# Scores of the last 64 keys as float32 products of two pairs at once

## The chip, the core and the metric

The kernel runs on one core of one Trainium2 chip. The metric is the device time of one execution in microseconds (us), lower is better. The engines are TensorE (PE for its products, PEld for its loads of weights into the array), ScalarE (ACT), VectorE (DVE), GpSimd (POOL, hardly used here) and SyncE (SP), which issues nearly all DMA transfers.

## The reference

Attention with a sigmoid in place of the softmax, then two matrix products with a leaky ReLU between them. There are 8 batches of 12 heads, 448 tokens and 64 values per head; d_model is 768 and d_ff is 2048.

```python
scores = scale * np.matmul(q, k.transpose(0, 1, 3, 2)) - np.log(S)
attn = 1.0 / (1.0 + np.exp(-scores))
attn_out = np.matmul(attn, v)
x = attn_out.transpose(0, 2, 1, 3).reshape(B * S, H * D)
h = x @ w_in
out = np.maximum(0.01 * h, h) @ w_out
```

## The kernel before

**Two kinds of product.** Most operands are float32 values that are split in two: a high part of type float32r, made by a cast on ACT (sometimes DVE), and a low part, the value minus its high part, made by a subtraction on DVE. A product of two split operands is three float32r products: high by high, high by low and low by high. The products of the sigmoids with v are not split: both operands are plain float32, and each such product shows as two instructions in the profile.

**The attention stage** works on 48 pairs of heads (`Pair`, line 343). The 128 partitions of a pair's tile hold the 64 head values of its two heads, so a score product needs only half of the array's rows, and the two heads of a pair run in the two halves side by side. The 448 keys of a head are four chunks: three of 128 and one of 64. For each chunk six score products (three for each of two heads) fill a tile of PSUM, `sc`, of two banks, one for each head. ACT takes the sigmoid of it into a tile `s`. There are three such PSUM tiles (tag `s` of `ps_a`), and five tiles for sigmoids (pool `at`).

The last chunk has only 64 keys. An even pair (`part` 1) writes its scores to partitions 0 to 63 of its tile, an odd pair (`part` 2) to partitions 64 to 127 of another tile, for which it multiplies 128 keys and uses 64. Both sigmoids go to one tile `s`, so that the last keys of two pairs can be multiplied with v together: four float32 products, each in its own quarter of the array (64 rows by 64 columns), in `attn_v` of the odd pair.

**Order of the work.** The order of instructions on every engine is the order in which the program issues them. The program runs in slots: `slot` (line 108) first issues the chores that are due (`later`), then the slot's own products. Step j of the attention stage has four slots: the last two chunks of pair j's scores (`scores(1)`), the first two chunks of pair j+1 (`scores(0)`), then the products with v for chunks 0 and 1 (`attn_v(0)`) and for the rest (`attn_v(1)`). Chores of step j: the split of pair j+2 (`high` on ACT, or on DVE where ACT has another cast in that slot, and `low` on DVE), the load of v for pair j+2, and the load of q and k for pair j+4. These loads go to the pool `raws`, which has two tiles; the parts go to the pool `spl`, two tiles as well. The results of two pairs are copied from PSUM by ACT (`keep`) in the first slot behind the odd pair. Beside all this DVE prepares the weights (`prep`), a given number of operations in each slot, and at given slots (`PLAN_ATTN`) parts of the attention output are split for the stage that follows (`h` high, `l` low, `s` sum; "h602" is the high part of operand 6, all three blocks).

**The product stages** multiply the four quarters of the tokens with `w_in` and later with `w_out`, by a scheme of seven products for a two by two block product (`ORDER`, `Quad`). A quarter of the first one is 56 steps of nine products, eight groups of seven operands in the order 0, 1, 4, 5, 3, 6, 2. The operands of quarter p+1 are split while quarter p is multiplied, in steps named by `PLANS` ("p50" is step 50 of the quarter before, "np0" step 0 of the quarter itself).

**Places.** Operands and parts lie in tiles of one size, handed out by `take` from two lists, `left` and `right`, oldest first. The attention stage has LEFT = 10 left and RIGHT = 14 right tiles. When its own pools are closed, MORE = 4 left tiles are made in their place and join the end of the left list.

Of the kernel before, what the change touches and what calls it, by code (L numbers as in the profile page):

```python
# [9 lines left out]
F32 = mybir.dt.float32  # L10
F32R = mybir.dt.float32r
I32 = mybir.dt.int32
AF = mybir.ActivationFunctionType
# [3 lines left out]
P = 128  # L17
# [3 lines left out]
NOP = len(ORDER)  # L21
# [9 lines left out]
IDLE = 7  # L31


LEFT, MORE, RIGHT = 10, 4, 14


def part(i):
# [14 lines left out]
def attn_ffn_kernel(ctx: ExitStack, tc: tile.TileContext, qk, v, w_in, w_out, out):  # L52
# [13 lines left out]
    S = qk.shape[3]  # L66
    NP = qk.shape[0] // B
    D = P // 2
    NK = 4
# [4 lines left out]
    NQ = B // 2  # L74
    scale = 1.0 / math.sqrt(D)
    bias = -math.log(S)
    heads = [slice(j * D, j * D + D) for j in range(2)]
# [9 lines left out]
    mm, dma = pinned(nc.tensor.matmul), pinned(nc.sync.dma_start)  # L87
    copy, act, dma_act = (pinned(x) for x in (nc.scalar.copy, nc.scalar.activation, nc.scalar.dma_start))
# [3 lines left out]
    def sub(to, x, y):  # L92
        vec(out=to, in0=x, in1=y, op=ALU.subtract)
# [64 lines left out]
    class Quad:  # L158
# [14 lines left out]
        def take(self, what, acc, how=copy):  # L173
            t = self.pool.tile([P, S], F32, tag=self.tag, name=f"{what}_{self.name}", bufs=self.bufs)
            how(out=t, in_=acc[:, :S])
            return t
# [30 lines left out]
    ps = ExitStack()  # L207
# [22 lines left out]

    def tiles(stack, name, side, n):
        pool = stack.enter_context(tc.tile_pool(name=name, bufs=1, side=side, reuse_waits="tile"))
        free[side].extend((pool, f"{name}{i}", side) for i in range(n))

    taken = {}

# [10 lines left out]
    def give(name):  # L247
# [5 lines left out]
    tiles(left, "l", "left", LEFT)  # L253
    attn = ExitStack()
    raws, spl, at = (attn.enter_context(tc.tile_pool(name=name, bufs=bufs, reuse_waits="tile")) for name, bufs in (
        ("raws", 2), ("spl", 2), ("at", 5)))
    warm = shift(ctx, "warm", 32, "right")
    tiles(right, "r", "right", RIGHT)
    pp = right.enter_context(tc.tile_pool(name="pp", bufs=2, side="right"))
# [80 lines left out]
    HALVES = slice(0, S // 2), slice(S // 2, S)  # L340
    KEYS = slice(0, 2 * P), slice(2 * P, S)

    class Pair:


# [22 lines left out]

        def high(self, how=None):
            self.parts = spl.tile([P, 2, 2, S], F32R, tag="qks", name=f"qks_{self.i}")  # L370
            (how or copy)(out=self.parts[:, 0], in_=self.raw)

        def low(self):
            sub(self.parts[:, 1], self.raw, self.parts[:, 0])

        def split(self):

            self.parts = spl.tile([P, 2, 2, S], F32R, tag="qks", name=f"qks_{self.i}")
            high, low = self.parts[:, 0], self.parts[:, 1]
            for cols in HALVES:  # L380
                copy(out=high[:, 0, cols], in_=self.raw[:, 0, cols])
            for n, cols in enumerate(KEYS):
                vcopy(out=high[:, 1, cols], in_=self.raw[:, 1, cols])
                sub(low[:, 1, cols], self.raw[:, 1, cols], high[:, 1, cols])
                if n == 0:
                    for x in HALVES:
                        sub(low[:, 0, x], self.raw[:, 0, x], high[:, 0, x])

        def scores(self, h):
            todo, acts = [], []  # L390
            for c in range(2 * h, 2 * h + 2):
                ps = psum("s", f"sc_{self.i}_{c}")

                if c < NK - 1:
                    k0, n, rows = c * P, P, slice(0, P)
                elif self.part == 1:
                    k0, n, rows = S - D, D, slice(0, D)
                else:
                    k0, n, rows = S - P, P, slice(D, P)

                for cols in HALVES if self.i == h == 0 else (slice(0, S),):
                    for m, (kp, qp) in enumerate(((0, 0), (0, 1), (1, 0))):
                        for j, me in enumerate(heads):
                            todo.append((c, (m > 0 and c + 1, m, cols.start), dict(
                                out=ps[:n, j, cols], lhsT=self.parts[me, kp, 1, k0:k0 + n],
                                rhs=self.parts[me, qp, 0, cols], start=m == 0 and cols.start == 0,
                                stop=m == 2 and cols.stop == S, skip_group_check=True)))
                acts.append((c, rows, ps))
            if self.i == h == 0:
                todo.sort(key=lambda x: x[1])  # L410
            for n, (c, rows, ps) in enumerate(acts):
                for x in todo if self.i == h == 0 and n == 0 else [x for x in todo if x[0] == c and (self.i or h)]:
                    mm(**x[2])
                if self.part == 2 and c == NK - 1:
                    s = pairs[self.i - 1].a[c]
                else:
                    s = at.tile([P, 2, S], F32, tag="s", name=f"s_{self.i}_{c}")
                act(out=s[rows], in_=ps[rows, :, :S], func=AF.Sigmoid, bias=bias, scale=scale)
                self.a.append(s)

        def attn_v(self, h):
            if h == 0:
                self.pv = psum("pv", f"pv_{self.i}")
            for c in range(2 * h, min(2 * h + 2, NK - 1)):
                for j, me in enumerate(heads):
                    mm(self.pv[me, :S], lhsT=self.v[:, (NK - 1) * j + c, :], rhs=self.a[c][:, j], start=c == 0, stop=False,
                       skip_group_check=True)
            if h == 1 and self.part == 2:
                x = pairs[self.i - 1]
                for j, me in enumerate(heads):  # L430
                    for y, rows in ((x, heads[0]), (self, heads[1])):
                        mm(y.pv[me, :S], lhsT=self.v[rows, 2 * NK - 2 + j, :], rhs=self.a[NK - 1][rows, j],
                           start=False, stop=True, skip_group_check=True)
                later(1, x.keep, self.keep, first=True)

# [9 lines left out]
    class Operands:  # L445
# [3 lines left out]
        def __init__(self, p):  # L449
            self.p, self.hi, self.lo, self.s2, self.got = p, {}, {}, None, set()  # L450

            self.sides = ("right", "left")[p == NQ - 1:]

        def x(self, i):
            return xs[4 * self.p + i]
# [5 lines left out]

        def high(self, n, a, b):
            if n not in self.hi:
                self.hi[n] = take(f"hi{n}_{self.p}", F32R, self.sides)
            copy(out=self.hi[n][:, a:b], in_=self.of(n)[:, a:b])

        def low(self, n, a, b):
            if n not in self.lo:
                self.lo[n] = take(f"lo{n}_{self.p}", F32R, self.sides)
            sub(self.lo[n][:, a:b], self.of(n)[:, a:b], self.hi[n][:, a:b])  # L470
            if b == NB and n not in (0, 1):
                assert self.got >= {4: {2, 4}, 5: {2}, 3: {1}, 6: {1, 2}, 2: {4}}[n]
                give(f"s2_{self.p}" if n == 4 else f"x_{4 * self.p + {5: 0, 3: 2, 6: 3, 2: 1}[n]}")
# [22 lines left out]
        def do(self, what):  # L496
# [6 lines left out]

    PLAN_ATTN = {
# [3 lines left out]
    COMMON = {  # L508
        "p12": "h002", "p13": "l002", "p14": "s302", "p19": "h102", "p20": "l102", "p21": "s202", "p27": "s402", "p36": "s102",
        "p33": "h402"}  # L510
    PLANS = (
        {}, dict(COMMON, p50="h502", p51="l402", p54="h302", p55="l502 h602", np0="l302", np1="l602", np2="h202", np3="l202"),
        dict(COMMON, p34="l402", p40="h502", p41="l502", p54="h302", p55="l302 h602", np0="l602", np2="h202", np3="l202"),
        dict(COMMON, p0="x002", p3="x202", p7="x102", p10="x302", p34="l402", p40="h502", p41="l502", p54="h302",
             p55="l302 h602", np0="l602", np2="h202", np3="l202"))


# [112 lines left out]
    def go(todo, work, pace=0):  # L630
# [5 lines left out]
        slot(work)  # L636
        prepare(pace)

    unread = psum("s", "unread")[:, 0]
    for _ in range(IDLE):  # L640
        mm(unread[heads[0], :S // 4], lhsT=zeros[:, :D], rhs=zeros, start=True, stop=True)
    slot(lambda: pairs[0].scores(0))
    for j in range(last + 1):
        works = [lambda: pairs[j].scores(1)] + [lambda: pairs[j + 1].scores(0)] * (j < last)
        works += [lambda: pairs[j].attn_v(0), lambda: pairs[j].attn_v(1)]
        if j + 2 <= last:
            later(0, pairs[j + 2].load_v)

            later(1, lambda j=j: pairs[j + 2].high(vcopy if PLAN_ATTN.get(f"e{j}.1", "").startswith("h") else copy))
            later(2, pairs[j + 2].low)  # L650
        if j + 4 <= last:
            later(4, pairs[j + 4].load_qk)
        for n, work in enumerate(works):
            go([(ops[0], PLAN_ATTN.get(f"e{j}.{n}", ""))], work, PACES[0] * (j > 0))

            t = EARLY.get((j - last, n))
            if t is not None:
                advance(t)
# [174 lines left out]
```

## Time and profile before

| | |
|---|---|
| median of 3 runs | 1088.2 us (1088.03 to 1088.58) |
| profiled execution | 1088.8 us, its span 1086.9 us |
| granted clock of TensorE | 1.000 |
| PE busy | 1080.6 us (99% of the span) |
| DVE busy | 677.4 us (62%) |
| ACT busy | 607.9 us (56%) |
| attention stage | from 0 to about 275.8 us |
| product stages | from about 275.8 to 1086.9 us |

The profile is of one execution. A row of the timeline gives the start and the length of a run of like instructions, then engine, line, operation, the tiles (`out<-in`), the shape, the count, and in brackets the idle time ahead of it with what ended it. All operations go through one helper, so every row has line 85; the tiles tell them apart: `sc` scores in PSUM, `s` sigmoids, `pv` the products with v, `qk` raw q and k, `qks` their parts, `hi` and `lo` the parts of the operands, `px`, `py`, `pz` the sums of the product stages. The length of a product in a row holds the time in which it passes through the array, so a busy PE can still be waiting within it; the starts of the weight loads (PEld) tell more. "issue" means that the engine waited for nothing that the profile shows.

### The profile page before, as it was taken

The page shows a single profiled execution, that of the slowest core. Times are in us where ns is not written, and L with a number is a line of the kernel's source. Part 1 is how long each engine was busy: PE and PEld are TensorE (multiplying, and loading weights), DVE is VectorE, ACT ScalarE, POOL GpSimd, SP SyncE. Part 2 cuts the span into 40 slices and gives each one's busy share as a digit, 9 for nine tenths or more (in the row PEclk, how much of TensorE's full clock was granted, in tenths as well). Part 3 has the DMA queues.
Part 4 walks back from the last instruction along what each step waited for, and adds up shares of the span by engine and source line. Part 5 has one row for each costly group of instructions (what it writes and reads, how often), then busy time and mean ns, then how long its engine had stood idle before and what let it go on. Part 6 is the DMA issues. An engine that isn't in the chain of part 4 may idle for free.

```text
span 1086.9 us, 16262 instructions
## 1 busy us (share of the span) xinstructions
PE 1080.6 (99%) x5978; PEld 897.5 (83%) x5978; DVE 677.4 (62%) x1022; ACT 607.9 (56%) x855; POOL 0.3 (0%) x5
## 2 busy tenths in 40 slices
PE   9999999999999999999999999999999999999998
PEld 5554555545899999999999999999999999999997
DVE  5667787776598789878887666565432423242332
ACT  7888888888555655565556555554333232323231
POOL 0000000000000000000000000000000000000000
PEclk9999999999999999999999999999999999999999
DMA  7677778778889889989887888886654554455452
GB/s 247 233 281 261 248 238 284 262 256 311 250 258 309 250 252 320 277 281 355 278 272 251 271 289 268 295 275 215 191 156 123 168 167 154 131 176 160 147 157 87
DMA packets 107792, 255.61 MB, mean 235 GB/s; under 512 B 11969, under 2 KB 55745, under 8 KB 107713
## 3 DMA queue, kind: packets, MB, share of 16 engines
q1 hardware_dynamic: 107280, 254.13, 71.8%
q8 instruction: 46, 0.75, 0.3%
q10 hardware_dynamic: 432, 0.46, 0.1%
q14 instruction: 34, 0.27, 0.1%
HBM read 167.38 MB, written 87.16 MB: 234 GB/s over the span
## 4 chain that ended last, share of the span: by engine, by line
PE 98%; DMA 1%; DVE 0%; SPq 0%; issue 0%; ACT 0%; ACTq 0%; DVEq 0%
PE px_o L85 21%; PE px_h L85 21%; PE pv L85 13%; PE sc L85 12%; PE pz_o L85 11%; PE pz_h L85 10%; PE py_o L85 5%; PE py_h L85 5%; DMA g<-s 1%; DMA qk<-in_qk 0%; DVE qks L85 0%; SPq L85 0%; DVE w L85 0%; ACTq L85 0%; ACT c_h L85 0%
## 5 line engine op out<-in xcount | busy, mean ns | idle before, releaser
L85 DVE TENSOR_TENSOR gs<-gg,gs 128x896 fp32r<-128x896 f32 x112 | 122.4, 1093 | 226.8 <-ACT gs L85 226.6
L85 PE MATMUL px_h<-hi,w 128*128 128x448 f32 x768 | 232.6, 363 | 0.6 <-ACT c_h L85 0.6
L85 PE MATMUL px_o<-gs,w 128*128 128x448 f32 x1152 | 232.5, 362 | 0.0
L85 ACT CAST gs<-gg 128x896 fp32r<-128x896 f32 x112 | 105.6, 943 | 222.8 <-PE px_o L85 115.9
L85 PEld LDWEIGHTS px_o<-gs,w 128*128 128x128 f32 x1152 | 216.0, 187 | 14.4
L85 ACT ACTIVATE s<-sc 128x896 f32<-128x896 f32 x192 | 168.0, 917 | 26.3 <-PE sc L85 24.8
L85 PEld LDWEIGHTS px_h<-hi,w 128*128 128x128 f32 x768 | 144.1, 188 | 11.0 <-ACT c_h L85 0.9
L85 PEld LDWEIGHTS sc<-qks 64*128 64x128 f32 (+1 forms) x1164 | 97.2, 178 | 56.3 <-ACT s L85 29.0
L85 PE MATMUL pv<-s,v 128*64 128x448 f32 (+1 forms) x768 | 140.7, 551 | 0.0
L85 DVE TENSOR_TENSOR w<-wx,w 128x768 fp32r<-128x768 f32 (+1 forms) x160 | 136.0, 852 | 4.8 <-ACT w L85 4.2
L85 PE MATMUL px_h<-lo,w 128*128 128x448 f32 x384 | 138.2, 360 | 0.0
L85 PE MATMUL sc<-qks 64*128 64x448 f32 (+2 forms) x1164 | 136.7, 378 | 1.1 <-DVE qks L85 1.0
L85 ACT CAST w<-wx 128x768 fp32r<-128x768 f32 (+1 forms) x160 | 119.5, 750 | 5.0 <-DMA wx<-t 5.0
L85 PE MATMUL pz_h<-hi,w 128*128 128x448 f32 x384 | 118.7, 363 | 0.0
L85 PE MATMUL pz_o<-gs,w 128*128 128x448 f32 x576 | 116.5, 362 | 0.0
L85 PEld LDWEIGHTS pz_o<-gs,w 128*128 128x128 f32 x576 | 108.0, 187 | 7.2
L85 PEld LDWEIGHTS pv<-s,v 128*64 128x64 f32 (+1 forms) x768 | 42.1, 135 | 76.0 <-issue 76.0
L85 DVE TENSOR_TENSOR qks<-qk,qks 128x896 fp32r<-128x896 f32 (+3 forms) x51 | 52.7, 1036 | 59.1 <-ACT qks L85 59.0
L85 ACT COPY c_h<-px_h 128x448 f32<-128x448 f32 x64 | 34.1, 534 | 95.1 <-PE px_h L85 87.5
L85 PEld LDWEIGHTS px_h<-lo,w 128*128 128x128 f32 x384 | 71.8, 187 | 5.1
L85 PEld LDWEIGHTS pz_h<-hi,w 128*128 128x128 f32 x384 | 72.1, 188 | 4.7
L85 DVE SCALAR_TENSOR_TENSOR wd<-wr,wd 128x384 int32<-128x384 int32 x128 | 71.2, 557 | 3.3
(47 smaller groups left out, 923.2 us busy)
## 6 DMA issues: line engine op xcount, KB each, us to landing
gg<-g SPq DMA_DIRECT2D x112, 448.0 KB, 3.5
wx<-t SPq DMA_DIRECT2D x120, 384.0 KB, 4.5
g<-c_h SPq DMA_DIRECT2D x128, 224.0 KB, 4.6
g<-s SPq DMA_DIRECT2D x96, 224.0 KB, 4.5
qk<-in_qk SPq DMA_DIRECT2D x46, 448.0 KB, 4.6
wr<-in_w_in SPq DMA_DIRECT2D x32, 384.0 KB, 3.8
t<-ws SPq DMA_DIRECT2D x16, 768.0 KB, 6.5
wr<-in_w_out SPq DMA_DIRECT2D x32, 384.0 KB, 3.9
```

What stands on the lines that cost most here:

```text
L85: return lambda *args, **kw: tc.keep_in_program_order(issue(*args, **kw))
```

## The change

The scores of the last 64 keys are taken from `scores`, for all pairs. A new function `last_scores` computes them for two pairs at once: four float32 products straight from the raw q and k, unsplit, each in a quarter of the array, into one PSUM tile, and one sigmoid over all 128 partitions. They are issued behind `attn_v(1)` of the odd pair before (a new function `ending`), and for the first two pairs behind `attn_v(1)` of pair 0. The splits leave out the last 64 columns of k (`SPLIT`, 832 of 896 columns).

Since the raw q and k are now read later, `raws` has four tiles, and `at` has six. For their room LEFT goes from 10 to 8 and MORE from 4 to 6, so in the attention stage two places fewer are to be had: the parts of operands 6 and 2 of quarter 0 are made in steps 0 to 3 of the product stage and not in steps 36 to 41 of the attention stage, and lie in the new left tiles. New tiles are put ahead of the list, and the low part of operand 5 of quarter 3 is made at step 52, not 41.

```diff
-LEFT, MORE, RIGHT = 10, 4, 14
+LEFT, MORE, RIGHT = 8, 6, 14
...
-        free[side].extend((pool, f"{name}{i}", side) for i in range(n))
+        free[side][:0] = [(pool, f"{name}{i}", side) for i in range(n)]
...
-        ("raws", 2), ("spl", 2), ("at", 5)))
+        ("raws", 4), ("spl", 2), ("at", 6)))
...
+    SPLIT = slice(0, 2 * S - D)
+
+    def flat(x):
+        return x.rearrange("p a s -> p (a s)")[:, SPLIT]
...
-            (how or copy)(out=self.parts[:, 0], in_=self.raw)
+            (how or copy)(out=flat(self.parts[:, 0]), in_=flat(self.raw))
...
-            sub(self.parts[:, 1], self.raw, self.parts[:, 0])
+            sub(flat(self.parts[:, 1]), flat(self.raw), flat(self.parts[:, 0]))
...
-            for n, cols in enumerate(KEYS):
+            for n, cols in enumerate((KEYS[0], slice(2 * P, S - D))):
...
-            for c in range(2 * h, 2 * h + 2):
+            for c in range(2 * h, min(2 * h + 2, NK - 1)):
...
+        def attn(self, c, ps):
+            s = at.tile([P, 2, S], F32, tag="s", name=f"s_{self.i}_{c}")
+            act(out=s, in_=ps[:, :, :S], func=AF.Sigmoid, bias=bias, scale=scale)
+            return s
+
+        def last_scores(self):
+
+            ps = psum("s", f"sc_{self.i}_{NK - 1}")
+            for j, me in enumerate(heads):
+                for y, rows in zip(pairs[self.i:], heads):
+                    mm(ps[rows, j, :S], lhsT=y.raw[me, 1, S - D:], rhs=y.raw[me, 0], start=True, stop=True, skip_group_check=True)
+            self.last = self.attn(NK - 1, ps)
...
-                        mm(y.pv[me, :S], lhsT=self.v[rows, 2 * NK - 2 + j, :], rhs=self.a[NK - 1][rows, j],
+                        mm(y.pv[me, :S], lhsT=self.v[rows, 2 * NK - 2 + j, :], rhs=x.last[rows, j],
...
-            self.sides = ("right", "left")[p == NQ - 1:]
+            self.sides = [SIDES[p == 0 and n in (6, 2)][p == NQ - 1:] for n in range(NOP)]
...
-        "e36.1": "h602", "e38.1": "l602", "e39.1": "h202", "e41.1": "l202"}
...
-        {}, dict(COMMON, p50="h502", p51="l402", p54="h302", p55="l502 h602", np0="l302", np1="l602", np2="h202", np3="l202"),
+        {"np0": "h602", "np1": "l602", "np2": "h202", "np3": "l202"},
...
-p34="l402", p40="h502", p41="l502", p54="h302",
+p34="l402", p40="h502", p52="l502", p54="h302",
...
+    def ending(j):
+
+        pairs[j].attn_v(1)
+        x = 0 if j == 0 else j + 1
+        if x % 2 == 0 and x < last:
+            pairs[x].last_scores()
...
-        works += [lambda: pairs[j].attn_v(0), lambda: pairs[j].attn_v(1)]
+        works += [lambda: pairs[j].attn_v(0), lambda: ending(j)]
```

More of the change, by code (lines that the diff above doesn't have):

```diff
@@ L390, in scores @@
             todo, acts = [], []
-            for c in range(2 * h, 2 * h + 2):
+            for c in range(2 * h, min(2 * h + 2, NK - 1)):
                 ps = psum("s", f"sc_{self.i}_{c}")
[L394 to L399, printed above, removed]
                 for cols in HALVES if self.i == h == 0 else (slice(0, S),):
@@ L404, in scores @@
                             todo.append((c, (m > 0 and c + 1, m, cols.start), dict(
-                                out=ps[:n, j, cols], lhsT=self.parts[me, kp, 1, k0:k0 + n],
+                                out=ps[:, j, cols], lhsT=self.parts[me, kp, 1, c * P:c * P + P],
                                 rhs=self.parts[me, qp, 0, cols], start=m == 0 and cols.start == 0,
                                 stop=m == 2 and cols.stop == S, skip_group_check=True)))
-                acts.append((c, rows, ps))
+                acts.append((c, ps))
             if self.i == h == 0:
                 todo.sort(key=lambda x: x[1])
-            for n, (c, rows, ps) in enumerate(acts):
+            for n, (c, ps) in enumerate(acts):
                 for x in todo if self.i == h == 0 and n == 0 else [x for x in todo if x[0] == c and (self.i or h)]:
                     mm(**x[2])
[L414 to L419, printed above, removed]
+                self.a.append(self.attn(c, ps))
+        def attn(self, c, ps):
[8 more added lines that the diff above has]
+            self.last = self.attn(NK - 1, ps)
         def attn_v(self, h):
@@ L463, in high @@
             if n not in self.hi:
-                self.hi[n] = take(f"hi{n}_{self.p}", F32R, self.sides)
+                self.hi[n] = take(f"hi{n}_{self.p}", F32R, self.sides[n])
             copy(out=self.hi[n][:, a:b], in_=self.of(n)[:, a:b])
@@ L468, in low @@
             if n not in self.lo:
-                self.lo[n] = take(f"lo{n}_{self.p}", F32R, self.sides)
+                self.lo[n] = take(f"lo{n}_{self.p}", F32R, self.sides[n])
             sub(self.lo[n][:, a:b], self.of(n)[:, a:b], self.hi[n][:, a:b])
@@ L505, in attn_ffn_kernel @@
         "e13.1": "h002", "e15.1": "l002", "e17.1": "h102", "e19.1": "l102", "e20.1": "s302", "e22.1": "s202", "e24.1": "s402",
[2 rows of a table removed]
+        "e26.1": "s102", "e27.1": "h402", "e29.1": "l402", "e30.1": "h502", "e32.1": "l502", "e33.1": "h302", "e35.1": "l302"}
     COMMON = {
@@ L511, in attn_ffn_kernel @@
     PLANS = (
-        {}, dict(COMMON, p50="h502", p51="l402", p54="h302", p55="l502 h602", np0="l302", np1="l602", np2="h202", np3="l202"),
+        {"np0": "h602", "np1": "l602", "np2": "h202", "np3": "l202"},
+        dict(COMMON, p50="h502", p51="l402", p54="h302", p55="l502 h602", np0="l302", np1="l602", np2="h202", np3="l202"),
         dict(COMMON, p34="l402", p40="h502", p41="l502", p54="h302", p55="l302 h602", np0="l602", np2="h202", np3="l202"),
-        dict(COMMON, p0="x002", p3="x202", p7="x102", p10="x302", p34="l402", p40="h502", p41="l502", p54="h302",
+        dict(COMMON, p0="x002", p3="x202", p7="x102", p10="x302", p34="l402", p40="h502", p52="l502", p54="h302",
              p55="l302 h602", np0="l602", np2="h202", np3="l202"))
```

1 row of the table PLAN_ATTN is left out of this document.

## The prediction

> **What bounds the kernel now.** I read the page first, then the busy time by stage, then the order of PE's work in the attention stage, and last the weight loads (PEld), whose start times show where PE's array really pauses.
>
> ```profile
> span 1086.9 us, 16262 instructions
> PE 1080.6 (99%) x5978; PEld 897.5 (83%) x5978; DVE 677.4 (62%) x1022; ACT 607.9 (56%) x855; POOL 0.3 (0%) x5
> PE 98%; DMA 1%; DVE 0%; SPq 0%; issue 0%; ACT 0%; ACTq 0%; DVEq 0%
> 0.00:275.77 275.77, 273.62 (x1946) 141.81 (x1946) 197.19 (x361) 232.16 (x290) 0.30 (x5) 1.00 0.76 261
> 217.56:228.80 11.24, 11.24 (x82) 5.78 (x80) 9.82 (x19) 9.51 (x13) 0.00 (x0) 1.00 0.52 153
> 228.80:240.05 11.25, 11.25 (x82) 5.79 (x81) 7.71 (x13) 9.89 (x13) 0.00 (x0) 1.00 1.00 367
> ```
>
> In the window rows the columns after the length are PE, PEld, DVE, ACT and POOL busy, then the granted clock, the DMA share and GB/s. PE is busy throughout and is 98% of the chain, at clock 1.00. The attention stage, which holds all edited products, is the first 275.77 us. ACT (9.5 to 9.9 us) and DVE (9.82 in its fullest cycle) fit within a cycle of 11.25 us. The DMA engines are full in some cycles (1.00) and half idle in others (0.52).
>
> ```profile
> 15.14 3.39 PE L85 MATMUL pv<-s,v 128*64 128x448 f32 x20
> ...
> 130.91 2.85 PE L85 MATMUL sc<-qks 64*128 64x448 f32 x24
> 133.68 2.48 PE L85 MATMUL pv<-s,v 128*64 128x448 f32 x12
> 136.09 2.83 PE L85 MATMUL sc<-qks 64*128 64x448 f32 x24
> 138.84 3.39 PE L85 MATMUL pv<-s,v 128*64 128x448 f32 x20
> ...
> 262.54 3.39 PE L85 MATMUL pv<-s,v 128*64 128x448 f32 x20
> ...
> 271.04 1.49 PE L85 MATMUL sc<-qks 64*128 64x448 f32 x12
> 272.45 3.39 PE L85 MATMUL pv<-s,v 128*64 128x448 f32 x20
> ```
>
> Two pairs make one cycle: from 15.14 to 262.54 there are 22, so 247.40/22 = 11.245 us each. A group of 24 score products (four chunks of keys) takes 2.77 us from start to start behind an odd pair (130.91 to 133.68) and 2.75 behind an even one (136.09 to 138.84). The last group has two chunks and takes 1.41 (271.04 to 272.45).
>
> ```profile
> 128.02 0.14 PEld L85 LDWEIGHTS pv<-s,v 128*64 128x64 f32 x2 [0.23 <-issue]
> ...
> 129.15 0.14 PEld L85 LDWEIGHTS pv<-s,v 128*64 128x64 f32 x2 [0.23 <-issue]
> 130.00 0.21 PEld L85 LDWEIGHTS pv<-s,v 64*64 64x64 f32 x8 [0.70 <-issue]
> 130.91 1.72 PEld L85 LDWEIGHTS sc<-qks 64*128 64x128 f32 x18 [0.70 <-issue]
> 132.88 0.50 PEld L85 LDWEIGHTS sc<-qks 64*128 64x128 f32 x6 [0.24 <-ACT s L85]
> ...
> 271.04 1.11 PEld L85 LDWEIGHTS sc<-qks 64*128 64x128 f32 x12 [0.70 <-ACT s L85]
> ```
>
> This view carries the sum. A float32 product is two passes, and the passes of the v products follow each other every 0.377 us (128.02 to 129.15 is three). The four quarter products with v that close an odd pair (eight loads at 130.00) take 0.91 us until the next group: two passes, 0.75, plus 0.16 at their borders. The six loads of the fourth score chunk start 0.24 us late, because its PSUM tile is freed only when ACT has read the first chunk: three tiles serve four chunks.
>
> **The change part by part.**
>
> *Removed chunks.* The loads of three chunks take 1.72 us and of two 1.11, so a chunk is 0.61. A group of three then takes 1.41 + 0.61 = 2.02 us. That saves 0.75 and 0.73, 1.48 per cycle, the 0.24 us wait included.
>
> *Added products* (call them L). Four float32 products, 64 rows by 64 columns each, one per quarter, 448 columns: the form of the four with v at 130.00, and like them each row half writes a bank of its own. They stand directly behind those four. Since the borders, not the passes, cost 0.16 there, and no border lies between two groups of one shape, I take two passes, 0.75; the other end is 0.91, as if they had borders of their own. A gain is excluded, since two passes cannot be less than 0.75 at these rows.
>
> Net per cycle 1.48 - 0.75 = 0.73 us, times 22 = **16.1 us**. The closing stretch from 262.54 gives 0.75 for its first group, 0.61 for its second (two chunks become one) and pays 0.75 for the last L: **+0.6**.
>
> *The beginning.*
>
> ```profile
> 7.75 0.47 PE L85 MATMUL sc<-qks 64*128 64x448 f32 x2 [0.41 <-DVE qks L85]
> 8.79 1.28 PE L85 MATMUL sc<-qks 64*128 64x448 f32 x10 [0.57 <-DVE qks L85]
> 6.98 0.63 DVE L85 CAST qks<-qk 128x896 fp32r<-128x896 f32 x1 [1.56 <-DMA qk<-in_qk]
> 7.64 1.09 DVE L85 TENSOR_TENSOR qks<-qk,qks 128x896 fp32r<-128x896 f32 x1
> ```
>
> Pair 0's fourth chunk ends before PE waits anyway for pair 1's split (7.75, 8.79), so dropping it gains nothing. Pair 1's chunk gives about 0.73, but the first L stands between products with v of another shape and scores, so it costs 0.91. The split of pair 1 is 832 instead of 896 columns, some 7% of 0.63 + 1.09, 0.1 us on the path. Together **-0.1**. With four raw buffers the loads of pairs 2 and 3 no longer wait, and join the queue behind pair 1's; I cost that at nothing, at worst some tenths if pair 1's data comes later.
>
> Sum: 16.1 + 0.6 - 0.1 = 16.6 us, before waits.
>
> *The PSUM wait.* L takes one of the three tiles, so an L and the three chunks behind it are again four in a row.
>
> ```profile
> 131.03 0.97 ACT L85 COPY x<-pv 128x448 f32<-128x448 f32 x2 [0.64 <-PE pv L85]
> 131.88 1.72 ACT L85 ACTIVATE s<-sc 128x896 f32<-128x896 f32 x2
> 133.50 0.93 ACT L85 CAST qks<-qk 128x896 fp32r<-128x896 f32 x1
> 134.46 1.09 DVE L85 TENSOR_TENSOR qks<-qk,qks 128x896 fp32r<-128x896 f32 x1 [0.28 <-ACT qks L85]
> ```
>
> Let T be the end of L, where the next score group starts. ACT follows a closing PE group by 0.12 us (130.91 to 131.03), a sigmoid is some 0.92 (two overlapped take 1.72), and today's waiting load starts 0.08 behind it (131.88 + 0.92 to 132.88). L's tile is free at T + 1.12; the third chunk's loads are due at about T + 1.11. So the wait shrinks from 0.24 to about nothing; bounds 0 and 0.24, and I take 0.05 for 23 groups, **1.2 us** lost. The other group of a cycle has only three chunks.
>
> *ACT and DVE.* ACT does seven sigmoids a cycle instead of eight and two shorter casts: 9.51 - 0.92 - 2 x 0.07 = 8.5 of some 10.5 us. The sigmoid of L is ahead of the two copies of the pairs' results, which move 0.9 later; the accumulator they free is wanted at T + 2.02, and the first copy ends near T + 1.5. Then a sigmoid and the cast of an even step end near T + 3.5, and DVE's low half near T + 4.6. It is needed about T + 2.02 + 2.41 (the products with v, 133.68 to 136.09) + 0.61 + 0.1 = T + 5.1. That slack was 1.6 us (135.55 against 136.09 + 1.11). I cost it at nothing; without cover each 0.1 us costs 2.3 over 23 cycles.
>
> *Buffers and queues.* A sixth sigmoid tile matches the six that are alive at once. A raw tile now stays until its L is done, but there are four: the wait on SP for load j+4 is for the L of pair j, at the end of step j-1 or earlier, instead of for the low half of pair j+2. Only load 4 comes later: the L of pairs 0 and 1 ends one score group of 2.0 us ahead of the products with v that start at 15.14 today, near 13.2. With the 4.6 us to landing (row below) it is there at 18, before its cast, some 2.6 us behind the second L, near 22. Behind it on SP stand loads of v and of raw weights, whose users come later still. The same bytes must pass in 16 us less; in cycles where the DMA engines are full already (1.00) a load may land later. All loads of pairs but that one may start earlier than today, so I cost it at nothing; if one came late, every 0.1 us would be seen once.
>
> *Four splits moved* into the first product steps (h6, l6, h2, l2 of quarter 0).
>
> ```profile
> qk<-in_qk SPq DMA_DIRECT2D x46, 448.0 KB, 4.6
> 281.48 0.53 ACT L85 COPY c_h<-px_h 128x448 f32<-128x448 f32 x1 [2.33 <-PE px_h L85]
> 297.05 1.32 ACT L85 CAST hi<-x 128x1344 fp32r<-128x1344 f32 x1
> 205.47 1.55 DVE L85 TENSOR_TENSOR lo<-x,hi 128x1344 fp32r<-128x1344 f32 x1
> 282.93 0.56 DVE L85 TENSOR_TENSOR w<-wx,w 128x384 fp32r<-128x384 f32 x1 [1.68 <-ACT w L85]
> 284.89 0.36 PE L85 MATMUL pz_h<-hi,w 128*128 128x448 f32 x1
> 286.69 0.36 PE L85 MATMUL px_h<-hi,w 128*128 128x448 f32 x1
> ```
>
> They take 2 x 1.32 us of ACT and 2 x 1.55 of DVE, in steps of 1.8 us (284.89 to 286.69) in which both idle (2.33 and 1.68 us ahead of the rows shown). The tightest is the last: behind the weight half of 282.93 it would end at 283.49 + 1.55 = 285.0, and operand 2 is first multiplied at about 286.7. Cost nothing; without that idle time at most about 3 us. The four freed slots in the attention stage only relieve ACT and DVE, save that two pairs' casts return from DVE to ACT (0.93 each), under PE. The half l502 of quarter 3 comes 11 steps later, still seven steps of 1.8 us before its use. The product stages keep their products: no term.
>
> **Sum:** 16.6 - 1.2 = 15.4 us. From the profiled execution's 1088.8 (1.9 above its span) that is 1073.4; it lies 0.6 above the median of the runs, 1088.2, so the forecast is **1072.8 us**.
>
> **The rivals.**
>
> *The wait stays.* If L's sigmoid comes late, the third chunk waits as the fourth does today, 0.24 x 23 = 5.5 instead of 1.2; if L also has borders of its own, 0.16 x 22 = 3.5 more. Time 1077 to 1080.6. For it: the margin of -0.01 us; against it: ACT's idle time, 0.64 us, just where L's sigmoid falls.
>
> *L runs two and two.* Its order puts the two products of one row half next to each other, those with v alternate the halves. If neighbours in one half didn't overlap, L would take four passes, 1.51: net -0.03 a cycle, and with the 0.94 lost in the beginning and 1.2 of waits nothing is gained, about 1091. Against it: the v products at 128.02 are neighbours on the same rows too, and run in pairs every 0.377 us. The Trainium skill, "TensorE: Matmul & The Clock Gate", Part 3, says that weight loads overlap running products only where the row group differs. By that rule each of L's passes would show 0.14 us of loads, 2 x 0.14 x 23 = 6.4 us in all, and the time would be 1079; the trace disagrees, for its v products, on all rows with 0.14 us loads, would then take over 0.5 us a pass, not 0.377.
>
> *Slower: the low halves come late.* The even step's slack falls from 1.6 to about 0.5 us, at DVE, which is in order and full of weight preparation. Once the half is on average 0.5 + 0.7 = 1.2 us later than its cast allows, each cycle loses more than it gained; at 1.5 us late the loss is 1.0 x 23 = 23 us, so 1096. For it: 9.82 us of DVE work against a cycle of 10.5. Against it: at 134.46 DVE had sat idle 0.28 us until ACT's cast was done, not the other way round.
>
> *The moved splits stall the first products:* 3 us, 1076.
>
> **How the numbers follow.** Forecast (1070 to 1075) 0.72; the wait stays 0.15; moved splits stall 0.05; two and two 0.04; late low halves 0.04. The low end, 1070.3, has no waits and 1 us of luck in the beginning; the high end, 1080, takes in the wait and the borders together. About 0.2%, 2.2 us, is what a measurement can tell from no change: faster 0.92 (the first three cases), slower 0.06, same 0.02 (the last two, whose times reach to the bound).
>
> **What would show it.** Score groups of 2.0 us start to start; the loads of L in one row together with those of the four with v, about 1.65 us until the next group; loads of the third chunk without a wait on ACT; a cycle of 10.5 us; the first px product near 260; product stages still about 811 us. Score groups over 2.2 us, L over 1 us, or a wait on qks in each cycle would make the prediction wrong.

## The result and the profile after

The changed kernel takes 1072.63 us (median of 4 runs, 1071.55 to 1073.21) against 1088.12 us before: a ratio of 0.9856, 95% interval 0.9839 to 0.9873. The forecast was 1072.8 us.

The page and the busy time by stage of the changed kernel (columns as before):

```profile
span 1071.4 us, 16068 instructions
PE 1063.9 (99%) x5882; PEld 884.1 (83%) x5882; DVE 672.2 (63%) x1020; ACT 581.4 (54%) x833; POOL 0.3 (0%) x5
PE 98%; DMA 1%; DVE 0%; SPq 0%; issue 0%; ACT 0%; ACTq 0%; DVEq 0%
...
0.00:259.23 259.23, 256.64 (x1850) 128.37 (x1851) 188.33 (x357) 203.27 (x266) 0.31 (x5) 1.00 0.79 276
259.23:1071.40 812.17, 807.24 (x4036) 755.69 (x4032) 483.89 (x664) 378.11 (x567) 0.00 (x0) 1.00 0.71 227
```

PE still bounds the kernel. The attention stage is 16.5 us shorter (275.77 to 259.23). The product stages are 1.0 us longer (1086.90 - 275.77 = 811.13, now 812.17). PE's order in the attention stage, from its timeline:

```profile
15.11 2.10 PE L85 MATMUL pv<-s,v 128*64 128x448 f32 x10
...
130.83 3.39 PE L85 MATMUL pv<-s,v 128*64 128x448 f32 x20
134.04 0.93 PE L85 MATMUL sc<-qk 64*64 64x448 f32 x8
134.90 2.09 PE L85 MATMUL sc<-qks 64*128 64x448 f32 x18
136.93 2.48 PE L85 MATMUL pv<-s,v 128*64 128x448 f32 x12
139.33 2.09 PE L85 MATMUL sc<-qks 64*128 64x448 f32 x18
141.35 3.01 PE L85 MATMUL pv<-s,v 128*64 128x448 f32 x16
...
246.57 3.39 PE L85 MATMUL pv<-s,v 128*64 128x448 f32 x20
```

The row `sc<-qk` is L, the four new products in two passes; the score groups have 18 products. The same stretch in the weight loads, with the loads of L behind the eight of the quarter products with v:

```profile
133.24 0.21 PEld L85 LDWEIGHTS pv<-s,v 64*64 64x64 f32 x8 [0.70 <-issue]
133.67 0.15 PEld L85 LDWEIGHTS sc<-qk 64*64 64x64 f32 x4 [0.22 <-issue]
134.04 0.15 PEld L85 LDWEIGHTS sc<-qk 64*64 64x64 f32 x4 [0.22 <-issue]
134.90 1.72 PEld L85 LDWEIGHTS sc<-qks 64*128 64x128 f32 x18 [0.71 <-issue]
136.92 0.20 PEld L85 LDWEIGHTS pv<-s,v 128*64 128x64 f32 x4 [0.30 <-ACT x L85]
```

The two quarter groups take 1.66 us together (133.24 to 134.90), against 0.91 for one before: L adds 0.75. Each score group takes 2.02 (134.90 to 136.92), and its 18 loads are one row without a pause. A cycle is (246.57 - 15.11)/22 = 10.52 us.

| stretch | before | after | difference | predicted |
|---|---|---|---|---|
| beginning, to the products with v of step 1 | 15.14 | 15.11 | -0.03 | +0.1 |
| 22 cycles | 247.40 | 231.46 | -15.94 | -16.1, and up to 1.2 of waits against it |
| close of the attention stage | 13.23 | 12.66 | -0.57 | -0.6 |
| product stages | 811.13 | 812.17 | +1.04 | 0 |

Where PE waits (engine, for whom, total, times, longest), first before, then after the change:

```profile
...
PE sc L85 <- DVE qks L85: 1.0, 2, 0.6
PE px_h L85 <- ACT c_h L85: 0.6, 1, 0.6
```

```profile
PE px_h L85 <- ACT c_h L85: 1.4, 1, 1.4
...
PE sc L85 <- ACT s L85: 0.8, 1, 0.8
PE sc L85 <- DVE qks L85: 0.5, 1, 0.5
...
```

The waits of `sc` and the rows left out are in the first 9 us. So there is one stall in the product stages, in both kernels, and it was 0.8 us longer in the changed one: most of the 1.04.

### The profile page after: what moved, and what is told of

Read it like the earlier page. It is cut to its first block, busy times and chain, and to the rows that moved or that the text cites. A ratio compares the mean times of both kernels' runs of the same rounds, so it can differ in the third digit from the quotient of the medians.

```text
span 1071.4 us, 16068 instructions
## 1 busy us (share of the span) xinstructions
PE 1063.9 (99%) x5882; PEld 884.1 (83%) x5882; DVE 672.2 (63%) x1020; ACT 581.4 (54%) x833; POOL 0.3 (0%) x5
## 4 chain that ended last, share of the span: by engine, by line
PE 98%; DMA 1%; DVE 0%; SPq 0%; issue 0%; ACT 0%; ACTq 0%; DVEq 0%
PE px_o L85 22%; PE px_h L85 21%; PE pv L85 13%; PE pz_o L85 11%; PE sc L85 11%; PE pz_h L85 10%; PE py_o L85 5%; PE py_h L85 5%; DMA g<-s 1%; DMA qk<-in_qk 0%; DVE qks L85 0%; SPq L85 0%; DVE w L85 0%; ACTq L85 0%; ACT c_h L85 0%
## 5 line engine op out<-in xcount | busy, mean ns | idle before, releaser
L85 ACT ACTIVATE s<-sc 128x896 f32<-128x896 f32 x168 | 150.2, 934 | 48.1 <-PE sc L85 48.1
L85 PEld LDWEIGHTS sc<-qks 64*128 64x128 f32 x876 | 76.5, 186 | 42.1 <-issue 31.7
L85 PE MATMUL sc<-qks 64*128 64x448 f32 (+1 forms) x876 | 101.5, 373 | 1.6 <-ACT s L85 0.8
L85 DVE TENSOR_TENSOR qks<-qk,qks 128x832 fp32r<-128x832 f32 (+3 forms) x51 | 49.5, 973 | 57.1 <-ACT qks L85 57.0
```

Of the source, the lines that this page charges most:

```text
L85: return lambda *args, **kw: tc.keep_in_program_order(issue(*args, **kw))
```

## The experiments

Diffs are from the changed kernel unless the text says otherwise; times are medians, and every ratio is to runs of the kernel before on the same chip.

### Where the new products stand

```diff
     def ending(j):
-        pairs[j].attn_v(1)
         x = 0 if j == 0 else j + 1
         if x % 2 == 0 and x < last:
             pairs[x].last_scores()
+        pairs[j].attn_v(1)
```

> The four float32 score products (L) are issued ahead of attn_v(1) of the odd pair, not behind it; nothing else changes. Theory: every group of products of another shape pays 0.15 to 0.16 us at its borders, and L pays none only because it stands right behind the four quarter products with v. Ahead of attn_v(1) it splits the products with v in two groups and stands alone: 2 x 0.155 us more per cycle, 23 cycles, 7.1 us: 1079.7 us, with L alone 0.91 us from its first load to the next group. Rival, the place does not matter: 1072.6 us.

Measured: 1079.75 us (1079.5 to 1081.31), ratio 0.9923 to the kernel before (0.9908 to 0.9937). Its weight loads:

```profile
135.92 0.14 PEld L85 LDWEIGHTS pv<-s,v 128*64 128x64 f32 x2 [0.23 <-issue]
136.77 0.21 PEld L85 LDWEIGHTS sc<-qk 64*64 64x64 f32 x8 [0.70 <-ACT s L85]
137.68 0.20 PEld L85 LDWEIGHTS pv<-s,v 128*64 128x64 f32 x4 [0.70 <-issue]
...
138.58 0.21 PEld L85 LDWEIGHTS pv<-s,v 64*64 64x64 f32 x8 [0.70 <-issue]
139.50 1.72 PEld L85 LDWEIGHTS sc<-qks 64*128 64x128 f32 x18 [0.70 <-ACT s L85]
```

L alone takes 0.91 us (136.77 to 137.68), the last two products with v 0.90 instead of 0.75, and the quarter group its 0.92. So each of these groups of float32 products pays 0.15 to 0.16 us at its border to products of another tile shape, and "next to those with v" is worth 7 of the 15.5 us. The page "TensorEngine Tiling (Array Packing)" of the Trainium skill, "Key Properties", says that a change of the tiling mode drains the array; the 0.15 to 0.16 us of this run fit that. Not every change of shape shows such a price, though: in the kernel before, the score group at 130.91 has 64x64 products in its middle and took 2.77 us, the one at 136.09 has none and took 2.75. Why those don't pay is open.

### The order of the four

```diff
-            for j, me in enumerate(heads):
-                for y, rows in zip(pairs[self.i:], heads):
+            for y, rows in zip(pairs[self.i:], heads):
+                for j, me in enumerate(heads):
...
```

> The two loops around the four products of L change places, so that the neighbours alternate the row halves like those with v. Theory: the four quarters run at once whatever their order; 1072.6 us within 1 us, and the loads of L again 0.37 us after those of the products with v. Rival (order matters, and the measured order is the lucky one): four passes for L, 0.75 us x 23 = 17 us more, about 1090 us.

Measured: 1072.35 us (1071.74 to 1073.14), ratio 0.9852 (0.9837 to 0.9867). The loads of L come in fours 0.38 us apart, as before. The order of the products over the quarters makes no difference, and the rival "two and two" falls.

### Only two quarters at a time

```diff
...
     def ending(j):
...
+        if two:
+            pairs[x].last_scores(0)
         pairs[j].attn_v(1)
...
+        if two:
+            pairs[x].last_scores(1)
```

`two` is the condition that stood ahead of `last_scores()`. The first call issues the two products of the first pair, the second those of the other pair and the sigmoid.

> L is cut in two: the two products of the first pair ahead of attn_v(1), those of the second pair behind it; one tile and one sigmoid as before. So only two quarters of the array work at a time on the last keys. Theory: two products take as long as four, two passes; the first half costs 0.91 us with borders, and the products with v are split, 0.15 more: 1.06 x 23 = 24 us, 1097 us, so that nothing is left of the gain. Rival, half the products take half the time: about 0.45 us less per cycle than that, 1086 us.

Measured: 1097.54 us (1097.01 to 1099.27), ratio 1.0085 (1.007 to 1.01).

```profile
135.69 0.19 PEld L85 LDWEIGHTS sc<-qk 64*64 64x64 f32 x4 [0.70 <-ACT s L85]
136.59 0.20 PEld L85 LDWEIGHTS pv<-s,v 128*64 128x64 f32 x4 [0.70 <-issue]
137.50 0.21 PEld L85 LDWEIGHTS pv<-s,v 64*64 64x64 f32 x8 [0.70 <-issue]
137.94 0.14 PEld L85 LDWEIGHTS sc<-qk 64*64 64x64 f32 x2 [0.24 <-issue]
138.31 0.14 PEld L85 LDWEIGHTS sc<-qk 64*64 64x64 f32 x2 [0.24 <-issue]
```

Two products take 0.90 us alone (135.69 to 136.59), what four take. Of the 25 us lost against the changed kernel, two passes more in 23 cycles are 0.75 x 23 = 17; the other 7 or so are the borders, as in the run with L moved. So float32 instead of three split products is no gain in itself; the gain comes from four quarters working at once. The place beside a group of the same shape adds to it but is no condition: with L standing alone the kernel was still 9 us faster than the one before (1079.75 against 1088.89 on the same chip).

### The side edits alone

```diff
-LEFT, MORE, RIGHT = 10, 4, 14
+LEFT, MORE, RIGHT = 8, 6, 14
...
-        ("raws", 2), ("spl", 2), ("at", 5)))
+        ("raws", 4), ("spl", 2), ("at", 6)))
...
```

These edits are to the kernel before. The new left tiles go ahead of the list, and the plans of the splits and their sides are those of the change.

> The kernel before with only the side edits: four raw tiles, six sigmoid tiles, LEFT 8 and MORE 6, the splits h6, l6, h2, l2 of quarter 0 in the product stage, l502 of quarter 3 at step 52. Scores and splits of the pairs as before. Theory: they cost and bring nothing in the attention stage (its end stays at 275.8 us within 0.4), and in the product stages at most the 1.0 us that the changed kernel lost there (812.2 instead of 811.1): 1088 to 1089.2 us. Rival, the deeper buffers carry part of the gain: attention stage shorter by 1 us or more, time below 1087.

Measured: 1088.25 us (1087.97 to 1091.48), ratio 0.9999 (0.9989 to 1.0008). The attention stage ends with this row:

```profile
272.65 3.39 PE L85 MATMUL pv<-s,v 128*64 128x448 f32 x20
```

That is 0.2 us later than before (272.45). Deeper buffers, moved splits and new places bring and cost nothing that can be measured. The run doesn't hold the raw q and k until L, since it has no L. In this profile PE had no stall at all in the product stages, with the moved splits in them: the longer stall of the changed kernel isn't theirs.

### The full split

```diff
-    SPLIT = slice(0, 2 * S - D)
+    SPLIT = slice(0, 2 * S)
...
-            for n, cols in enumerate((KEYS[0], slice(2 * P, S - D))):
+            for n, cols in enumerate(KEYS):
```

> The changed kernel, but the splits of the pairs take all 896 columns again, the last 64 keys included, though nothing reads those parts. Theory: 0.06 us more for each cast and each low half lies under PE in all steps but the beginning, where it costs 0.1 us: 1072.7 us, cycle 10.52. Rival, the shorter splits carry part of the gain, through ACT and DVE: 0.12 us per pair, 5 us more.

Measured: 1073.35 us (1072.51 to 1074.93), beside 1073.43 for the changed kernel on the same chip. In PE's timeline a score group is again 2.02 us from its start to the next products with v (135.35 to 137.37):

```profile
135.35 2.09 PE L85 MATMUL sc<-qks 64*128 64x448 f32 x18
137.37 2.48 PE L85 MATMUL pv<-s,v 128*64 128x448 f32 x12
```

The shorter splits lie under PE, and the rival (5 us more) falls.

### The wait for the sigmoid of L

First the sigmoid of L was put behind the two copies of the pairs' results on ACT.

```diff
-            self.last = self.attn(NK - 1, ps)
+            later(1, lambda: setattr(self, "last", self.attn(NK - 1, ps)))
```

> The sigmoid of L is issued behind the two copies of the pairs' results on ACT, not ahead of them. Theory: the third chunk's loads have next to no margin against L's sigmoid (they start 0.08 us late and are just hidden), so 0.97 us of copies ahead of it shows as about 0.85 us of wait in each of 22 or 23 cycles: 18.5 to 20 us more, about 1092 us, with a wait on ACT s ahead of six loads of each group behind an L. Rival, the three PSUM tiles leave more room than that: 1072.6 us.

Measured: 1073.3 us (1072.35 to 1074.13), ratio 0.9863 (0.9846 to 0.9879). The expectation was wrong, and ACT's timeline says why:

```profile
134.21 0.97 ACT L85 COPY x<-pv 128x448 f32<-128x448 f32 x2 [1.16 <-PE pv L85]
135.07 1.74 ACT L85 ACTIVATE s<-sc 128x896 f32<-128x896 f32 x2
```

The copies need only the products with v. Ahead of the sigmoid they run while PE is still at L (the next score group began at 134.84), and the sigmoid starts 0.23 us behind L's end as in the changed kernel. Nothing was delayed, so the margin wasn't tested. A second run put the sigmoid behind that of the next chunk as well:

```diff
-            self.last = self.attn(NK - 1, ps)
+            later(2, lambda: setattr(self, "last", self.attn(NK - 1, ps)), first=True)
```

> The sigmoid of L is issued one slot later still: behind the two copies and behind the sigmoid of the next chunk. In the run before this the copies cost nothing, since ACT did them while PE was still at L. Theory: a full sigmoid of another chunk, which itself waits for that chunk's products, can't hide there: L's PSUM tile comes free about 2.8 us behind the start of the score group, while the third chunk's loads are due at 1.2, so some 1.5 us of wait on ACT s in each of 23 cycles, 34 us more, about 1106 us. Rival, the tile of L is not what the third chunk waits for: 1073 us.

Measured: 1090.09 us (1088.62 to 1091.15), ratio 1.0013 (1.0003 to 1.0023).

```profile
131.60 0.15 PEld L85 LDWEIGHTS sc<-qk 64*64 64x64 f32 x4 [0.22 <-issue]
132.46 1.11 PEld L85 LDWEIGHTS sc<-qks 64*128 64x128 f32 x12 [0.70 <-ACT x L85]
134.41 0.50 PEld L85 LDWEIGHTS sc<-qks 64*128 64x128 f32 x6 [0.84 <-ACT s L85]
135.22 0.20 PEld L85 LDWEIGHTS pv<-s,v 128*64 128x64 f32 x4 [0.31 <-issue]
```

```profile
131.83 0.97 ACT L85 COPY x<-pv 128x448 f32<-128x448 f32 x2 [1.16 <-PE pv L85]
133.44 1.73 ACT L85 ACTIVATE s<-sc 128x896 f32<-128x896 f32 x2 [0.64 <-PE sc L85]
```

The third chunk's loads now come 0.84 us late, the group takes 2.76 instead of 2.02 (132.46 to 135.22), and 0.74 x 23 = 17 us, all the gain, is gone. Half of what was expected: the loads at 134.41 start right behind the end of the first sigmoid (133.44 + 0.92 = 134.36), ahead of the end of L's, which is the second of that row (133.44 + 1.73 = 135.17). So the third chunk takes a tile that comes free earlier, no longer L's. That a late sigmoid holds up the third chunk's loads is shown, and so is that the group has no more than about 0.1 us to spare (0.84 us late cost 0.74).

### The stall in the product stages

Two kernels moved the four loads of quarter 3's rows within quarter 2, one by each of these edits.

```diff
-        dict(COMMON, p0="x002", p3="x202", p7="x102", p10="x302", p34="l402", p40="h502", p52="l502", p54="h302",
+        dict(COMMON, p0="x002", p2="x202", p4="x102", p6="x302", p34="l402", p40="h502", p52="l502", p54="h302",
...
-        dict(COMMON, p0="x002", p3="x202", p7="x102", p10="x302", p34="l402", p40="h502", p52="l502", p54="h302",
+        dict(COMMON, p0="x002", p4="x202", p10="x102", p15="x302", p34="l402", p40="h502", p52="l502", p54="h302",
```

> In the product stage of quarter 2 the four loads of quarter 3's rows (672 KB each) come at steps 0, 2, 4, 6, ahead of the steps that prepare weights, not at 0, 3, 7, 10. Theory: the single stall of PE in the product stages (step 11 of quarter 2, 0.5 to 1.5 us, while ACT waits for the store of a sum) comes from these loads in a DMA queue that is full; moved away from it, the stall goes, 0.5 to 1.4 us less: 1071.4 to 1072.0 us, and product stages of 811.2 us or a little less. Rival, the stores are late for another reason: the stall stays, 1072.6 us.

> The same four loads at steps 0, 4, 10, 15 of quarter 2. Theory: the loads spread over more steps, and none falls in the 4 steps ahead of step 11: the stall goes, 1071.4 to 1072.0 us, unless the last two loads bring a stall of their own at steps 12 to 17. Rival: 1072.6 us with the stall at step 11.

Measured: 1072.15 us (1072.02 to 1073.2), ratio 0.9851, and 1072.13 us (1071.73 to 1072.5), ratio 0.985. Both medians lie 0.1 us above the range that was expected. The second was run again beside the changed kernel:

> The changed kernel as it is, once more, beside the other runs of this call. Theory: 1072.6 us; PE's stall at step 11 of quarter 2 is there in the profile, 0.5 to 1.5 us long, and differs from execution to execution, so that the times spread over 1 to 1.5 us.

> The kernel with the four loads of quarter 3's rows at steps 0, 4, 10, 15, once more beside the changed kernel. Theory: no stall in the product stages, 0.5 to 1.0 us below the changed kernel of the same call. Rival, no difference.

Measured: 1073.43 us (1072.46 to 1073.66) for the changed kernel and 1072.04 us (1071.3 to 1073.92) with the loads moved. The row of ACT's timeline at that place, first in the changed kernel of this comparison, then with the loads at steps 0, 4, 10, 15 and at 0, 2, 4, 6:

```profile
482.16 0.53 ACT L85 COPY c_h<-px_h 128x448 f32<-128x448 f32 x1 [4.99 <-DMA g<-s]
```

```profile
479.89 0.53 ACT L85 COPY c_h<-px_h 128x448 f32<-128x448 f32 x1 [2.33 <-PE px_h L85]
```

```profile
480.68 0.53 ACT L85 COPY c_h<-px_h 128x448 f32<-128x448 f32 x1 [3.26 <-DMA g<-s]
```

In the first ACT waits 4.99 us for a store of a sum to free the tile it copies to, PSUM isn't freed, and PE stands for 1.5 us. With the loads at 0, 4, 10, 15 ACT waits for PE, as it should, in both runs; with the loads at 0, 2, 4, 6 it still waits for the store, but for 3.26 us only. PE's waits in the product stages are none in all three profiles.

The unmoved loads gave the stall in eight of ten profiles (the kernel before, the changed one and the runs above), 0.5 to 1.6 us long. In all eight it is ACT's wait at this place less 3.5 us: 0.47 us where ACT waited 3.98, 1.36 at 4.87, 1.61 at 5.12. In the two profiles without it (the side edits alone, two quarters at a time) ACT waited 2.82 and 2.83 us for the store. So the place and the mechanism of the stall are shown: ACT waits for a store, and PE stands once that wait is longer than about 3.5 us. (In the run with the order changed the profile puts the 4.17 us of ACT's wait down to PE, not to the store.) That the four loads hold up the store is not shown: the waits with the loads moved, up to 3.26 us, reach above the shortest with the loads unmoved. That moving them makes the kernel faster is likely, 0.5 us below the first runs of the changed kernel and 1.4 below those on the same chip, but the ranges overlap.

## Why the prediction was right

**The removed chunks** (0.75 and 0.73 us, a group of three at 2.02) were right to the hundredth: the steady groups take 2.02 or 2.03. The sum rested on the groups of three and two chunks that the trace of before already held.

**L at two passes without borders** was right: 0.75, and 0.91 when it stands elsewhere. The prediction took the 0.75 by reasoning from the borders; the run with L moved showed it.

**The PSUM wait** was mis-sized: 1.2 us were taken off, and the steady groups lost nothing. ACT started 0.23 us behind L's end (134.90 to 135.13), not 0.12, so L's tile was even later than worked out. The third chunk's loads did wait for it: they start at 136.10, right behind that sigmoid's end (135.13 + 0.92 = 136.05). The loads ahead of them came every 0.20 us (135.62, 135.82), so their time was 136.02. The sigmoid, and the first of those loads:

```profile
135.13 0.92 ACT L85 ACTIVATE s<-sc 128x896 f32<-128x896 f32 x1 [2.02 <-PE sc L85]
```

```profile
136.10 0.32 PEld L85 LDWEIGHTS sc<-qks 64*128 64x128 f32 x4
```

The group took 2.02 all the same: a load runs ahead of its product, and 0.08 us of lateness is hidden there. The step that was wrong is to count a late load as lost time. That the margin is thin was right: with L's sigmoid two slots later each group behind an L lost 0.74 us to such a wait, where the rival "the wait stays" had 0.24.

**ACT and DVE** were right at nothing. The low half of an even step starts at 138.52 and takes 1.03, so it ended 3.62 + 1.03 = 4.65 us behind L's end at 134.90, where 4.6 was worked out:

```profile
132.65 1.02 DVE L85 TENSOR_TENSOR qks<-qk,qks 128x832 fp32r<-128x832 f32 x1
138.52 1.03 DVE L85 TENSOR_TENSOR qks<-qk,qks 128x832 fp32r<-128x832 f32 x1 [1.39 <-ACT qks L85]
```

The odd step's row, at 132.65, has no idle time ahead of it: there DVE was late, the cast having ended at 131.48. It cost nothing, since those parts are wanted only by the group at 134.90. "Slower, the low halves come late" didn't happen.

**Buffers, queues, moved splits** at nothing: right. For the buffers and the splits the run with them alone shows it. For the raw tiles that are held until L it is the trace of the changed kernel: behind the first 9 us PE waits for no part of q or k, and the first product steps have no wait either.

**The product stages at nothing** is the step that failed. The prediction looked only at what the change puts into them, not at a stall that was already there (0.6 us in the profile of before) and that differs from profile to profile, from none to 1.6 us, with ACT's wait for a store. It was 1.4 us in the profiled execution. Whether the change itself made it longer is not shown. That the forecast came out exact is luck: this 1.0 us and the 1.2 us of waits that didn't come cancel. The sum of the products alone, 16.6 us before waits, was right: the attention stage is 16.5 us shorter.

The rule of the Trainium skill that the prediction set against the trace ("TensorE: Matmul & The Clock Gate", Part 3: weight loads overlap running products only of another row group) isn't borne out by L either: the loads at 133.67 lie under the last pass of the four products with v, those at 134.04 under L's first pass, in the same quarters, and the passes stay 0.37 apart.

## What to carry to other kernels

Price a removed piece from groups of the same kernel that already have the smaller size, and an added one from the start times of the weight loads, border and passes apart; busy times of overlapping products hide both. Float32 in quarters of the array paid here because four products ran at once, which was worth all of the gain; standing beside others of the same tile shape was worth nearly half of it. Look in the untouched stages too for a wait on a transfer: here it moved by more than a microsecond between kernels that differ elsewhere.

## What the runs showed that was not expected

Copies issued ahead of a sigmoid on an in-order engine cost nothing, as the engine was idle while PE did the products that the sigmoid waits for.

The loads of q and k took longer to land: a median of 5.4 us instead of 4.6. The side edits alone did it, with the old scores and the old 261 GB/s in the attention stage:

```profile
qk<-in_qk SPq DMA_DIRECT2D x46, 448.0 KB, 5.5
```

In the changed kernel, with 276 GB/s there, the median is no longer than that:

```profile
qk<-in_qk SPq DMA_DIRECT2D x46, 448.0 KB, 5.4
```

So the later landing comes with the side edits, not with the shorter time for the same bytes; with which of them is open. ACT's casts waited 3.4 us for such loads in all, 0.4 before and not at all with the side edits alone. PE did not wait for them behind the beginning.
